# Attention with a forget gate and a SwiGLU FFN in one kernel: the first 256 queries of batch 0 ahead of the rest, and its row sums turned by TensorE

## The chip, the core and the metric

The kernel runs on one core of a Trainium2 chip. A core has five engines with queues of their own: TensorE (PE in the profile; PEld is its weight load), VectorE (DVE), ScalarE (ACT), GpSimd (POOL) and SyncE (SP, which here only issues DMAs). Each queue is worked off in order, and engines wait for one another through semaphores. Sixteen DMA engines are shared by all queues. TensorE writes into PSUM, here eight banks of 128 x 512 floats.

The metric is the device time of the whole program in microseconds (us), as the median of several runs. A profile is one more execution, with its own time.

## The reference, cut to what matters

Eight batches of eight heads, 576 tokens, head size 64. Attention has a causal mask and a decay made of the cumulative sum of log f. The output of attention, 4608 tokens by 512, goes through an FFN of inner size 1536.

```python
scores = q @ k.T / 8
cum = np.cumsum(np.log(np.clip(f, 1e-4, 1.0)), axis=-1)
scores = np.where(causal, -1e9, scores + cum[..., :, None] - cum[..., None, :])
attn = np.exp(scores - max); attn = attn / (attn.sum(-1) + 1e-9)
x = (attn @ v).transpose(0, 2, 1, 3).reshape(4608, 512)
g = x @ w_gate
out = (g * sigmoid(g) * (x @ w_val)) @ w_out
```

## The kernel before

The order of all work on every queue is written out by hand. The unit is a *slot*: one bank of scores of one head. A head has four banks (`BANKS`), since only the causal blocks are computed: bank 0 holds queries 0 to 255 (384 columns in all), banks 1 to 3 the queries 256 to 575 (512, 384 and 320 columns). Head h, bank i is slot 4h + i, so 64 heads are 256 slots and a batch is 32. A dictionary `todo` maps a slot to functions and their arguments; the loop at the end calls them slot by slot, and after them as many matmuls of the FFN as the slot's share is.

- `load`, `cast`, `transposes` bring in a pair of heads: SP loads q, k and v as f32, POOL casts to bf16 (DVE casts v for the first five pairs), PE turns q and k with an identity (L131), ACT copies q and DVE copies k from PSUM into the tile `QK` (L136, L138). Three `QK` tiles rotate.
- The decay rides in four more rows of `QK`, so that the score matmul adds it. At the start `dec` is computed on DVE and ACT; ACT issues four small DMAs that write the rows of the first pair, and one that writes `dec` to DRAM, from where `rows` fetches those of later pairs (SP).
- `qk` (L151) makes a bank of scores on PE, ACT takes the exponential into `pt` (L157), POOL masks the diagonal block (L166). `pv` (L181) follows three slots later (`LAG`). The value tile has a column of ones, so row 64 of the result is the row sum. The results go from PSUM to `ev` (L192 on DVE, L194 on ACT).
- The division goes by groups of four heads. `collect` spreads a group's sums over 128 partitions by DMA (`sc`), `recip` takes the reciprocal on DVE, `back` writes it to DRAM (`rc_d`), `spread` reads it back to 64 partitions (`rb`), all issued on ACT's queue. `normalise` (L221) multiplies on DVE into `xT`, the FFN's input. For the last head of a group these stand 5, 10, 11, 16 and 21 slots (`NORM`, then one slot for each head) after that head's first slot plus `LAG`.
- `ffn_stream` works off nine tiles of 512 tokens: twelve times four matmuls for gate (`gp`, L235) and four for value (`vp`, L243), with Tanh on ACT (L238) and two products on DVE (L239, L246), then four output blocks of twelve matmuls (`fo`, L252), copied by ACT to `ot` and stored by SP. Its PSUM pool `ps_ffn` has four banks; `ps_s` has two, `ps_t` and `ps_o` one each. A tile has 144 matmuls and is spread over 32 slots; the first begins at slot 56.
- POOL issues the weight loads, which cast to bf16 on the way: gate and value in quarters at slots 8, 10, 16, 18 up to 34, the output weights in halves at 36 and 40.

Of the kernel before, what the change touches and what calls it, by code (L numbers as in the profile page):

```python
# [11 lines left out]
ALU = mybir.AluOpType  # L12
# [15 lines left out]
FEW = 5  # L28
NORM = 21
# [3 lines left out]
def kernel(ctx, tc, q, k, v, f, w_gate, w_val, w_out, out):  # L33
# [23 lines left out]
    ptp = ctx.enter_context(tc.tile_pool(name="ptp", bufs=3))  # L57
    evp = ctx.enter_context(tc.tile_pool(name="evp", bufs=3))
# [10 lines left out]
    NBUF = 3  # L69

    QK = [consts.tile([KR, 4, NB * P], BF16, name=f"QK{i}") for i in range(NBUF)]
# [10 lines left out]
    def load(p, nm, part=0):  # L82
# [8 lines left out]
        if part == 0:  # L91
            nat[nm, p] = natp.tile([P, NB, 2, D], F32, name="nat_v", tag="nat_v")
# [18 lines left out]
    def cast(p, nm):  # L111
        if nm == "v":
            b = p % NBUF
            vn = nat.pop(("v", p))
            eng = nc.vector if p < FEW else nc.gpsimd
            eng.tensor_copy(VB[b][:, : NB - 1, :, :D], vn[:, : NB - 1])
            eng.tensor_copy(VB[b][:LAST, NB - 1, :, :D], vn[:LAST, NB - 1])
            return
        nc.gpsimd.tensor_copy(  # L119
            BF[nm, p % 2][:QP].rearrange("p t h d -> p h t d"),  # L120
            nat.pop((nm, p)).rearrange("p h (t d) -> p h t d", d=D),
        )

    def transposes(p, nm):
        w_ = 0 if nm == "q" else 1
        src = BF[nm, p % 2].rearrange("p t h d -> p t (h d)")
        pool, tag = (ps_s, "s") if p < FEW else (ps_t, "t")
# [4 lines left out]
        for a in range(2):  # L132
            dst = QK[p % NBUF][:D, 2 * a + w_, :S].rearrange("p (c n) -> p c n", n=QT)
            sr = t[a * D : (a + 1) * D, :S].rearrange("p (n c) -> p c n", n=QT)
            if p == 0 or nm == "q":
                nc.scalar.activation(dst, sr, AF.Copy)  # L136
            else:
                nc.vector.tensor_copy(dst, sr)  # L138
# [3 lines left out]
    def qk(h, i):  # L142
        b, j = (h // 2) % NBUF, h % 2
        if i == 0:
            PT[h] = ptp.tile([P, PT_W], BF16, name="pt", tag="pt")
        pt = PT[h]
        pool, tag = (ps_ffn, "f") if h < 2 * FEW else (ps_s, "s")
# [10 lines left out]
        if i == 0:  # L158
            diag = pt[:, : 2 * QSPLIT].rearrange("p (n x) -> p n x", x=QSPLIT)[:, :, :P]
            pat = [[0, 2], [1, P]]  # L160
        else:
            kt, q0, w = [x for x in BANKS[i] if x[1] == x[0] * P][0]
            lo = off + sum(x[2] for x in BANKS[i][: [y[0] for y in BANKS[i]].index(kt)])
            m = min(P, w)
            diag, pat = pt[:, lo : lo + m], [[1, m]]
        nc.gpsimd.affine_select(  # L166
            out=diag, in_=diag, pattern=pat, compare_op=ALU.is_ge, fill=0.0, base=0, channel_multiplier=-1,
        )

    def pv(h, i):  # L170
# [3 lines left out]
        if i <= 1:  # L174
            pool, tag = (ps_t, "t") if half == 0 else (ps_o, "o")
# [4 lines left out]
        for n, (kt, q0, w) in enumerate(BANKS[i]):  # L180
            nc.tensor.matmul(  # L181
                o[:, q0 - q_lo : q0 - q_lo + w], VB[b][:, kt, j, :], PT[h][:, c : c + w],
# [3 lines left out]
        if last:  # L186
# [4 lines left out]
            if h < H + GH or half == 1:  # L191
                nc.vector.tensor_copy(dst, o[: D + 1, :q_n])  # L192
            else:
                nc.scalar.activation(dst, o[: D + 1, :q_n], AF.Copy)  # L194
            O.pop((h, half))
# [31 lines left out]

    def ffn_stream():
        for t in range(NMT):
            ts = slice(t * MT, (t + 1) * MT)  # L230
            for fc in range(KF):
                fs = slice(fc * P, (fc + 1) * P)
                g_ = ps_ffn.tile([P, MT], F32, name="gp", tag="f")
                for ko in range(KD):
                    nc.tensor.matmul(g_, wg[:, ko, fs], xT[:, ko, ts], start=(ko == 0), stop=(ko == KD - 1))  # L235
                    if ko == KD - 1:
                        th = fp.tile([P, MT], F32, name="th", tag="th")
                        nc.scalar.activation(th, g_, AF.Tanh, scale=0.5)  # L238
                        nc.vector.scalar_tensor_tensor(out=th, in0=th, scalar=1.0, in1=g_, op0=ALU.add, op1=ALU.mult)  # L239
                    yield t  # L240
                v_ = ps_ffn.tile([P, MT], F32, name="vp", tag="f")
                for ko in range(KD):
                    nc.tensor.matmul(v_, wv[:, ko, fs], xT[:, ko, ts], start=(ko == 0), stop=(ko == KD - 1))  # L243
                    if ko == KD - 1:
                        h_ = hp.tile([P, MT], BF16, name="hh", tag="hh")
                        nc.vector.tensor_mul(h_, th, v_)  # L246
                        hh[fc] = h_
                    yield t
            for ms in range(MT // P):
                o = ps_ffn.tile([P, DM], F32, name="fo", tag="f")  # L250
                for fc in range(KF):
                    nc.tensor.matmul(o, hh[fc][:, ms * P : (ms + 1) * P], wo[:, fc, :],  # L252
                                     start=(fc == 0), stop=(fc == KF - 1))
                    if fc == KF - 1:
                        ot = op_.tile([P, DM], F32, name="ot", tag="ot")
                        nc.scalar.activation(ot, o, AF.Copy, scale=0.5)  # L256
                        r0 = t * MT + ms * P
                        nc.sync.dma_start(out=out[r0 : r0 + P, :], in_=ot)
                    yield t


    with tc.tile_pool(name="ini", bufs=1) as ini:
        lf = ini.tile([BH, S], F32, name="lf")
        nc.scalar.dma_start(out=lf, in_=f.rearrange("b h s -> (b h) s"))
        for p in range(2):
            load(p, "q")
            load(p, "k")
            for part in range(3):
                load(p, "v", part)
        ident = consts.tile([P, P], BF16, name="ident")  # L270
        make_identity(nc, ident[:, :])
        zero = ini.tile([BH, S], F32, name="zero")
        nc.gpsimd.memset(zero, 0.0)
        dec = ini.tile([BH, 2, 4, S], BF16, name="dec")
        nc.vector.memset(dec[:, 0, 1:], 1.0)
        nc.vector.memset(dec[:, 1, 0], 1.0)
        for nm in "qk":
            for i in range(2):
                nc.gpsimd.memset(BF[nm, i][QP:], 0.0)
        for i in range(NBUF):  # L280
            nc.gpsimd.memset(QK[i][:, 1::2, S:], 0.0)
            nc.gpsimd.memset(VB[i][:, :, :, D:], 1.0)
            nc.gpsimd.memset(VB[i][LAST:, NB - 1], 0.0)
        nc.vector.tensor_scalar(out=lf, in0=lf, scalar1=1e-4, scalar2=1.0, op0=ALU.max, op1=ALU.min)
        nc.scalar.activation(lf, lf, AF.Ln)
        cum = ini.tile([BH, S], F32, name="cum")
        nc.vector.tensor_tensor_scan(out=cum, data0=lf, data1=zero, initial=0.0, op0=ALU.add, op1=ALU.add)
        nc.scalar.activation(dec[:, 0, 0], cum, AF.Copy, scale=8.0)
        nc.vector.tensor_scalar_mul(dec[:, 1, 1], cum, -8.0)
# [3 lines left out]
        nc.vector.tensor_sub(dec[:, 1, 3], r1, dec[:, 1, 2])  # L293

        load(2, "q")
        load(2, "k")
        for r in range(4):
            nc.scalar.dma_start(
                out=QK[0][D + r : D + r + 1, :, :S], in_=dec[0:2, :, r]
            )  # L300
        nc.scalar.dma_start(out=dec_dram, in_=dec)
    fp = ctx.enter_context(tc.tile_pool(name="fp", bufs=3))
    hp = ctx.enter_context(tc.tile_pool(name="hp", bufs=14))
# [7 lines left out]

    for h in range(BH):
        for i in range(NSLOT):
            at(NSLOT * h + i, qk, h, i)
    for h in range(BH):
        s0 = NSLOT * h
        for i in range(NSLOT):
            at(s0 + i + LAG, pv, h, i)
        if h % GH == GH - 1:
            g = h // GH  # L320
            at(s0 + 5 + LAG, collect, g)
            at(s0 + 10 + LAG, recip, g)
            at(s0 + 11 + LAG, back, g)
            at(s0 + 16 + LAG, spread, g)
            for j in range(GH):
                at(s0 + NORM + LAG + j, normalise, g * GH + j)

    for p in range(NP):
        s0 = 2 * NSLOT * p
        for n, (nm, part) in enumerate((("q", 0), ("k", 0), ("v", 0), ("v", 1), ("v", 2))):  # L330
            if p > 2 or (p == 2 and nm == "v"):
                at(s0 - 24 + n + n // 2, load, p, nm, part)
        if p > 0:
            at(s0 - 10, rows, p)
        at(s0 - 11, cast, p, "q")
        at(s0 - 7, cast, p, "k")
        at(s0 - 4, cast, p, "v")
        at(s0 - 7, transposes, p, "q")
        at(s0 - 3, transposes, p, "k")
    def weights(t, src, lo, hi, cols):  # L340
        if cols:
            nc.gpsimd.dma_start(out=t[:, :, lo:hi], in_=src.rearrange("(ko p) n -> p ko n", p=P)[:, :, lo:hi])
# [57 lines left out]
```

The softmax here doesn't subtract the row's maximum and nothing guards it: scores larger than these inputs give would overflow.

## Time and profile before

| | |
|---|---|
| median of 5 runs | 457.51 us (455.73 to 457.89) |
| profiled execution: its own time | 456.28 us |
| its span, first to last instruction | 454.5 us |
| mean granted TensorE clock | 0.959 |
| PE busy | 412.4 us (91%) |
| DVE, ACT, POOL busy | 285.5, 264.3, 177.9 us (63%, 58%, 39%) |
| DMA | 54.01 MB, mean 119 GB/s |

"Busy" is the time in which an engine had an instruction in work. Matmuls overlap one another, so a PE that is busy is not a PE at its peak. The profile also has the span cut into 40 equal slices with a digit of busy tenths for each engine, windows of chosen length with busy time, granted TensorE clock and DMA share, the chain of waits that ended last, and groups of like instructions with the mean duration of one.

The costliest groups, with the number of instructions and the mean of one:

| line, engine, operation | count | mean |
|---|---|---|
| L157 ACT, exponential into pt | 256 | 503 ns |
| L166 POOL, mask of a diagonal block | 256 | 349 ns |
| L235, L243, L252 PE, FFN matmuls of 512 columns | 3 x 432 | 379 to 381 ns |
| L239, L246 DVE, the two FFN products | 2 x 108 | 686, 684 ns |
| L138 DVE and L136 ACT, k and q into QK | 62, 66 | 753, 644 ns |
| L221 DVE, the division into xT | 64 | 795 ns |
| L131 PE, bf16 transposes | 192 + 192 | 236, 233 ns |

### The profile page before, as it was taken

The page shows a single profiled execution, that of the slowest core. Times are in us where ns is not written, and L with a number is a line of the kernel's source. Part 1 is how long each engine was busy: PE and PEld are TensorE (multiplying, and loading weights), DVE is VectorE, ACT ScalarE, POOL GpSimd, SP SyncE. Part 2 cuts the span into 40 slices and gives each one's busy share as a digit, 9 for nine tenths or more (in the row PEclk, how much of TensorE's full clock was granted, in tenths as well). Part 3 has the DMA queues.
Part 4 walks back from the last instruction along what each step waited for, and adds up shares of the span by engine and source line. Part 5 has one row for each costly group of instructions (what it writes and reads, how often), then busy time and mean ns, then how long its engine had stood idle before and what let it go on. Part 6 is the DMA issues. An engine that isn't in the chain of part 4 may idle for free.

```text
span 454.5 us, 7457 instructions
## 1 busy us (share of the span) xinstructions
PE 412.4 (91%) x2576; PEld 227.1 (50%) x2576; DVE 285.5 (63%) x452; ACT 264.3 (58%) x522; POOL 177.9 (39%) x404
## 2 busy tenths in 40 slices
PE   0685586999999999999999999999999999999996
PEld 0353353545555555555555555555555544444442
DVE  6355535787478747874788467846784585670760
ACT  2875463666677667666766677667766622332331
POOL 9476753353544454445454545454544200000000
PEclk9989555999999999999999999999999999999999
DMA  9899999440694068506850775077204113101002
GB/s 203 177 235 210 200 237 220 103 95 23 183 211 107 18 187 206 112 12 192 194 124 8 197 189 127 3 202 187 52 3 123 34 44 100 46 1 69 25 1 92
DMA packets 69417, 54.01 MB, mean 119 GB/s; under 512 B 45188, under 2 KB 63620, under 8 KB 68292
## 3 DMA queue, kind: packets, MB, share of 16 engines
q1 hardware_dynamic: 57516, 38.33, 34.2%
q10 hardware_dynamic: 6072, 10.49, 9.9%
q0 software_dynamic: 5792, 4.72, 6.5%
q8 instruction: 20, 0.33, 0.3%
q14 instruction: 17, 0.14, 0.1%
HBM read 47.90 MB, written 10.17 MB: 128 GB/s over the span
## 4 chain that ended last, share of the span: by engine, by line
PE 78%; DMA 9%; DVE 8%; ACT 2%; issue 2%; SPq 0%; ACTq 0%; DVEq 0%
PE fo L252 21%; PE gp L235 19%; PE vp L243 18%; PE o L181 8%; PE s L151 8%; PE tp L131 4%; DVE QK L138 3%; DMA rb<-rc_d 3%; DMA rc_d<-rc 3%; DVE xT L221 1%; DMA sc<-ev 1%; DVE th L239 1%; DMA nat_q<-in_q_dram 1%; DVE ev L192 1%; ACT QK L136 1%
## 5 line engine op out<-in xcount | busy, mean ns | idle before, releaser
L157 ACT ACTIVATE pt<-s 128x384 bf16<-128x384 f32 (+2 forms) x256 | 126.2, 503 | 82.1 <-PE s L151 70.8
L166 POOL TENSOR_SCALAR_AFFINE_SELECT pt<-pt 128x128 bf16<-128x128 bf16 (+2 forms) x256 | 88.7, 349 | 183.6 <-ACT pt L157 182.6
L235 PE MATMUL gp<-xT,wg 128*128 128x512 bf16 x432 | 120.0, 381 | 0.5 <-DVE th L239 0.5
L243 PE MATMUL vp<-xT,wv 128*128 128x512 bf16 x432 | 119.6, 380 | 0.2 <-DVE hh L246 0.2
L239 DVE SCALAR_TENSOR_TENSOR th<-th,gp 128x512 f32<-128x512 f32 x108 | 74.1, 686 | 64.3 <-ACT th L238 63.8
L181 PE MATMUL o<-pt,VB 128*128 128x320 bf16 (+4 forms) x448 | 92.0, 276 | 21.2 <-DVE QK L138 7.6
L252 PE MATMUL fo<-wo,hh 128*128 128x512 bf16 x432 | 104.4, 379 | 0.0
L151 PE MATMUL s<-QK 68*128 68x320 bf16 (+4 forms) x448 | 92.4, 279 | 5.6 <-ACT QK L136 3.1
L238 ACT ACTIVATE th<-gp 128x512 f32<-128x512 f32 x108 | 64.3, 596 | 50.8 <-PE gp L235 43.1
L246 DVE TENSOR_TENSOR hh<-th,vp 128x512 bf16<-128x512 f32 x108 | 73.9, 684 | 8.3 <-PE vp L243 1.1
L151 PEld LDWEIGHTS <-QK 68*128 68x128 bf16 x448 | 45.6, 105 | 48.0 <-ACT QK L136 3.4
L181 PEld LDWEIGHTS <-VB 128*128 128x128 bf16 x448 | 41.5, 102 | 48.4 <-issue 12.1
L192 DVE COPY ev<-o 65x320 f32<-65x320 f32 (+1 forms) x76 | 35.3, 471 | 43.5 <-PE o L181 42.8
L221 DVE TENSOR_TENSOR xT<-ev,rb 64x576 bf16<-64x576 f32 x64 | 50.9, 795 | 14.6 <-DMA rb<-rc_d 13.5
L252 PEld LDWEIGHTS <-hh 128*128 128x128 bf16 x432 | 40.7, 97 | 38.3
L235 PEld LDWEIGHTS <-wg 128*128 128x128 bf16 x432 | 41.0, 98 | 37.4 <-issue 1.3
L243 PEld LDWEIGHTS <-wv 128*128 128x128 bf16 x432 | 40.3, 98 | 36.3 <-issue 1.0
L138 DVE COPY QK<-tp 64x576 bf16<-64x576 bf16 x62 | 46.7, 753 | 17.4 <-PE tp L131 16.7
L136 ACT ACTIVATE QK<-tp 64x576 bf16<-64x576 bf16 x66 | 42.5, 644 | 6.0 <-DMA QK<-dec 4.2
L256 ACT ACTIVATE ot<-fo 128x512 f32<-128x512 f32 x36 | 21.5, 597 | 35.4 <-PE fo L252 31.9
L119 POOL CAST b_q<-nat_q 96x768 bf16<-96x768 f32 x32 | 27.0, 844 | 0.1
L131 PE MATMUL tp<-ident,b_q 128*128 128x128 bf16 x192 | 17.9, 236 | 10.1 <-POOL b_q L119 10.1
(37 smaller groups left out, 151.9 us busy)
## 6 DMA issues: line engine op xcount, KB each, us to landing
nat_q<-in_q_dram SPq DMA_DIRECT2D x32, 288.0 KB
nat_k<-in_k_dram SPq DMA_DIRECT2D x32, 288.0 KB
rb<-rc_d ACTq DMA_DIRECT2D x16, 576.0 KB
out_dram<-ot SPq DMA_DIRECT2D x36, 256.0 KB
nat_v<-in_v_dram SPq DMA_DIRECT2D x64, 128.0 KB
wg<-in_moe_w_gate_dram POOLq DMA_DIRECT2D x4, 384.0 KB, 8.6
wv<-in_moe_w_val_dram POOLq DMA_DIRECT2D x4, 384.0 KB, 8.6
wo<-in_moe_w_out_dram POOLq DMA_DIRECT2D x2, 768.0 KB, 15.4
```

What stands on the lines that cost most here:

```text
L138: nc.vector.tensor_copy(dst, sr)
L151: nc.tensor.matmul(s[:, c : c + w], QK[b][:, 2 * j + 1, kt * P : (kt + 1) * P], QK[b][:, 2 * j, q0 : q0 + w], start=True, stop=True,)
L157: nc.scalar.activation(pt[:, off : off + c], s[:, :c], AF.Exp, scale=0.125)
L166: nc.gpsimd.affine_select(out=diag, in_=diag, pattern=pat, compare_op=ALU.is_ge, fill=0.0, base=0, channel_multiplier=-1,)
L181: nc.tensor.matmul(o[:, q0 - q_lo : q0 - q_lo + w], VB[b][:, kt, j, :], PT[h][:, c : c + w], start=(i <= 1 and n == 0), stop=(last and n = ...
L221: nc.vector.tensor_mul(xT[a * D : (a + 1) * D, (h % H) // 2, b0 : b0 + S], E[g][:D, j], RB[g][:, j])
L235: nc.tensor.matmul(g_, wg[:, ko, fs], xT[:, ko, ts], start=(ko == 0), stop=(ko == KD - 1))
L238: nc.scalar.activation(th, g_, AF.Tanh, scale=0.5)
L239: nc.vector.scalar_tensor_tensor(out=th, in0=th, scalar=1.0, in1=g_, op0=ALU.add, op1=ALU.mult)
L243: nc.tensor.matmul(v_, wv[:, ko, fs], xT[:, ko, ts], start=(ko == 0), stop=(ko == KD - 1))
L246: nc.vector.tensor_mul(h_, th, v_)
L252: nc.tensor.matmul(o, hh[fc][:, ms * P : (ms + 1) * P], wo[:, fc, :], start=(fc == 0), stop=(fc == KF - 1))
```

## The change

- **Order of slots in batch 0.** Bank 0 of all eight heads comes first, in slots 0 to 7; then banks 1 to 3 head by head, slots 8 to 31. From head 8 on all is as before. For the first eight slots `pv` follows two slots later (`LAG0`), scores go to `ps_ffn`, and the exponentials to tiles of their own (`pt0p`, four buffers), with two mask instructions instead of one.
- **Row sums of batch 0.** They no longer go by DMA. For each half of a head, `turn` makes PE turn the row of sums into columns (two or three small f32 transposes), DVE takes their reciprocals, and `turn_back`, one slot later, makes PE spread them over 64 partitions; DVE multiplies them into `xT`. The sums take the last columns of a PSUM bank of `ps_ffn`, the spread values its first ones.
- **FFN tiles.** The first tile of 512 tokens becomes two of 256. A tile begins in the slot in which its tokens are ready, and its columns are spread evenly up to the beginning of the next: slots 12 to 36, 37 to 84, then 85 to 116 and so on.
- **Row sums of later batches.** `collect`, `recip`, `back`, `spread` and `normalise` stand 2, 6, 7, 11 and 15 slots after the last `pv` of the group; before they stood 2, 7, 8, 13 and 18 slots after it.
- **Start and loads.** q and k of three pairs are loaded first, then v. One tile `QKA` holds four buffers, and four DMAs on SP's queue write the decay rows of all eight heads of batch 0. Memsets, casts and transposes of the first pairs are put in a new order, and a one-element exponential is run early. In later batches loads come 20 slots ahead instead of 24 and `rows` 16 slots ahead instead of 10.
- **Weights.** Gate and value in quarters at slots 1, 2, 4, 5, 7, 8, 10 and 11; output weights in quarters at 15, 18, 21 and 24.
- `hp` has 13 buffers instead of 14, `nat_v` two instead of three; DVE casts v for the four pairs of batch 0.

```diff
-FEW = 5
-NORM = 21
+LAG0 = 2
+    pt0p = ctx.enter_context(tc.tile_pool(name="pt0p", bufs=4))
+    eap = ctx.enter_context(tc.tile_pool(name="eap", bufs=3))
-    NBUF = 3
+    NBUF = 4
+    FB = H // 2
+    QKA = consts.tile([KR, NBUF, 4, NB * P], BF16, name="QK")
+    QK = [QKA[:, i] for i in range(NBUF)]
...
+    def turn(h, half):
+        n = QSPLIT if half == 0 else S - QSPLIT
+        RS[h, half] = rs = ps_ffn.tile([P, MT], F32, name="rs", tag="f")
+        RCP[h, half] = rc = rp.tile([P, 3], F32, name="rcp", tag="rcp")
+        ea = EA[h, half]
+        for c in range(0, n, P):
+            w, x = min(P, n - c), SUMS + c // P
+            nc.tensor.transpose(rs[:w, x : x + 1], ea[D : D + 1, c : c + w], ident_f[D : D + 1, D : D + 1])
+        full = n // P
+        nc.vector.reciprocal(rc[:, :full], rs[:, SUMS : SUMS + full])
+        if n % P:
+            nc.vector.reciprocal(rc[: n % P, full : full + 1], rs[: n % P, SUMS + full : SUMS + full + 1])
+
+    def turn_back(h, half):
+        n = QSPLIT if half == 0 else S - QSPLIT
+        rc, rs, ea = RCP.pop((h, half)), RS.pop((h, half)), EA.pop((h, half))
+        for c in range(0, n, P):
+            w = min(P, n - c)
+            nc.tensor.transpose(
+                rs[:D, c : c + w], rc[:w, c // P : c // P + 1].to_broadcast([w, D]), ident_f[:w, :w]
+            )
+        j, q0 = h % 2, QSPLIT * half
+        nc.vector.tensor_mul(xT[j * D : (j + 1) * D, h // 2, q0 : q0 + n], ea[:D, :n], rs[:D, :n])
...
+    TILES = [(0, QSPLIT), (QSPLIT, MT - QSPLIT)] + [(t0, MT) for t0 in range(MT, N_TOK, MT)]
...
+        for r in range(4):
+            nc.sync.dma_start(
+                out=QKA[D + r : D + r + 1, :, :, :S].rearrange("r b (j w) s -> r (b j) w s", w=2), in_=dec[:H, :, r]
+            )
...
+    def slot(h, i):
+        if h >= H:
+            return NSLOT * h + i
+        return h if i == 0 else H + (NSLOT - 1) * h + i - 1
...
+        if h < H:
+            for half, s in enumerate((slot(h, 0) + LAG0, slot(h, NSLOT - 1) + LAG)):
+                at(s + 1, turn, h, half)
+                at(s + 2, turn_back, h, half)
+                ready[half] = s + 3
+        elif h >= H and h % GH == GH - 1:
+            g = h // GH
+            s = slot(h, NSLOT - 1) + LAG
+            at(s + 2, collect, g)
+            at(s + 6, recip, g)
+            at(s + 7, back, g)
+            at(s + 11, spread, g)
+            for j in range(GH):
+                at(s + 15 + j, normalise, g * GH + j)
+            ready[1 + h // H] = s + 15 + GH
...
     for c in range(4):
         lo, hi = c * DFF // 4, (c + 1) * DFF // 4
-        at(NSLOT * (2 + 2 * c), weights, wg, w_gate, lo, hi, True)
-        at(NSLOT * (2 + 2 * c) + 2, weights, wv, w_val, lo, hi, True)
-    for c in range(2):
-        at(NSLOT * (9 + c), weights, wo, w_out, c * KF // 2, (c + 1) * KF // 2, False)
+        at(1 + 3 * c, weights, wg, w_gate, lo, hi, True)
+        at(2 + 3 * c, weights, wv, w_val, lo, hi, True)
+    for c in range(4):
+        at(15 + 3 * c, weights, wo, w_out, 3 * c, 3 * c + 3, False)
...
+    begin = [ready[0], ready[1]]
+    begin += [ready[1 + (t0 + n - 1) // S] for t0, n in TILES[2:]]
...
+        while nxt is not None and nxt[0] + 1 < len(begin) and s >= begin[nxt[0]]:
+            t = nxt[0]
+            if t != t_now:
+                t_now, done = t, 0.0
+            if done >= work[t] * (s + 1 - begin[t]) / (begin[t + 1] - begin[t]):
+                break
+            done += nxt[1]
+            nxt = next(ffn, None)
```

## The prediction, made before the changed kernel was run

> **What bounds the kernel now.** I read the 40 slices first, then the windows of the slow stage, then the chain of waits in order of time. In the slices, TensorE (PE) is nearly full from about 80 us to the end, and before that it is neither full nor at full clock:
>
> ```profile
> PE   0685586999999999999999999999999999999996
> PEclk9989555999999999999999999999999999999999
> DMA  9899999440694068506850775077204113101002
> ```
>
> One digit is 11.4 us. The seven slices that matter are the first ones: DMA at its limit, PE at 0 to 8 tenths, clock down to 5 tenths. The windows (engine busy us of 10, then clock, DMA share, GB/s) say the same in numbers:
>
> ```profile
> 50.00:60.00 10.00, 6.42 (x34) 3.68 (x33) 6.51 (x11) 5.00 (x10) 6.04 (x14) 0.50 1.22 210
> 60.00:70.00 10.00, 8.58 (x52) 5.62 (x50) 2.90 (x5) 5.47 (x11) 5.72 (x15) 0.50 1.17 233
> 70.00:80.00 10.00, 5.61 (x24) 2.85 (x23) 5.78 (x9) 3.93 (x8) 3.13 (x7) 0.50 1.11 223
> 80.00:90.00 10.00, 10.00 (x65) 5.58 (x64) 7.28 (x12) 6.85 (x15) 3.59 (x10) 1.00 0.35 88
> ```
>
> The chain (start, length, what) names the waits of that stage, in its answer for the first 128 us:
>
> ```profile
> 32.56 6.30 DMA sc<-ev
> 39.18 5.40 DMA rc_d<-rc
> 44.61 5.72 DMA rb<-rc_d
> 50.42 0.76 DVE xT L221
> ...
> 57.21 6.06 DMA rc_d<-rc
> 63.30 7.99 DMA rb<-rc_d
> 71.38 0.76 DVE xT L221
> ...
> 76.31 1.71 PE gp L235 x4
> ...
> 119.62 0.34 PE tp L131 x6
> ...
> 123.97 0.86 PE gp L235 x4
> ```
>
> Batch 0's row sums go out and come back by three small DMAs per group of four heads, each taking 5.4 to 8 us while the DMA engines are full; 31.5 us of the chain are these five. The first FFN matmul starts at 76.3 us, the second FFN tile at 124.0. From there PE alone sets the pace: the full chain has the next tile's first gp at
>
> ```profile
> 169.77 0.86 PE gp L235 x4
> ```
>
> so a batch is 45.8 us (169.77 - 123.97). That is 144 matmuls of 0.216 (0.86/4) = 31.1, 8 heads of 1.40 (the chain's pieces of 0.14 to 0.22 for four banks of scores and four of values) = 11.2, eight groups of transposes of 0.34 = 2.7: 45.0. This stage has nothing to give; the change must earn its time before 124.0.
>
> **The change part by part, in slots.** A slot is one bank of scores. Before, tile 0 is spread over slots 56 to 87 and tile 1 starts at slot 88. After, the half tile of tokens 0 to 255 fills slots 12 to 36, the half of 256 to 511 fills 37 to 84, and the 512-token tiles start at 85, 117 and so on, 32 slots each as before. So slot 85 after is slot 88 before, at 124.0. What follows is 454.5 - 124.0 = 330.5, plus the 0.75 head that three slots hold: 0.75 x (1.40 + 0.34) = 1.3. I sum the time to slot 85 in four pieces.
>
> *To the first score matmul: 16.3.* Before it is at 14.96. The decay rows of all eight heads are now four SP issues (ACT's four took 3.47 in all), behind fourteen loads in SP's queue; the last waits for DVE's last decay operation (ends 11.6 before) and for the three issues ahead. With a landing of 0 to 4.1 us (the lf load: issued 0.82, used 4.96) it is there at 14.6 to 18.7; I take 16.3. Behind these issues SP holds the V loads of pairs 2 and 3, used ten us later. The Exp table load (1.28) moves from behind the first score into a wait, so the first exponential ends about 17.4.
>
> *Slots 0 to 11: to 33.* GpSimd decides. Between the first exponential and head 7's mask it runs 16 selects of 0.357 = 5.7, two blanks of 0.20 + 0.63 + 0.46 = 2.6, two casts of 0.83 = 1.7, and four weight issues of 0.78 = 3.1, which now stand among the selects: 13.1, so 30.5. ACT has 7.9 and DVE 11.8 in that time. Head 7 then goes through PV 0.3, copy 0.42, turn, reciprocal (0.26 at most), turn back and product (half of 0.75): with hand-overs 2.5. First gp at 33.0 against 76.3. Bounds 31 to 36.
>
> *Slots 12 to 36: 34.* PE: 96 half-width matmuls of 0.108 = 10.4 and 24 of 0.216 = 5.2; 25 slots of 2 x 0.177 = 8.9; three transposes groups 1.0; six small f32 turns a head, 48 in all. No row has these. The nearest is the bf16 transpose: 0.34/6 = 0.057 in a row, 0.236 as a single record. I take 0.06 for a one-column turn and 0.14 for a turn back, 4.8 in all; the bounds are 2.7 and 11.3. Sum 30.3. To it 2.5 for the eight turns that wait behind DVE's copy (0.48, with the one operation of 0.38 before it) with everything on PE behind them, and 1.0 for a clock that starts low. ACT's sum is 20 and DVE's 20, so both are hidden. Range 31 to 40. The weights: issued from slots 1 to 24 instead of 8 to 40; at 8.6 us from issue to landing (the page's median) wv's last quarter is there near 44, used near 50; wo's quarters at 47 to 59, used from 56 to 60. The loads of batch 1 compete less, since SP now waits at the rows of pair 4 until PE has passed slot 13; behind that wait stand the loads of pair 5, used 16 slots later.
>
> The page "TensorE: Matmul & The Clock Gate", section "Part 4: PE-mode transpose", of the Trainium skill puts a transpose at some 275 ns in a kernel and says that it does not count as activity for the clock. This speaks against the change: 48 such turns would be 13.2 us and the final sum 8.4 us more. In this trace six transposes take 0.34 us at full clock, so I do not use it.
>
> *Slots 37 to 84: 50.* Here only half a tile lies under 48 slots of attention. PE has 48 x 0.354 + 15.6 + 12 x 0.34 = 36.7. ACT has more: 48 exponentials of 0.503 = 24.1, 12 copies of 0.644 = 7.7, nine of 0.376 = 3.4, twelve Tanh of 0.38 (between 0.376 at 256 and 0.436 at 320 columns) = 4.6, two of 0.597, and some 2.2 groups of three DMA issues (0.50 + 0.33 + 0.46) = 2.9: 43.9. Each of the 27 copies and Tanh stands behind a PE piece of its own slot, at 0.14 to 0.34 a wait: 6 more. Range 45 to 58. The rows of groups 2 and 3 still take the three DMAs, with four slots each instead of five; at 1.04 us a slot that is 4.2 us, and the DMA engines are no longer full.
>
> Sum: 33 + 34 + 50 + 330.5 + 1.3 = 448.8, 5.7 less than the span of 454.5. The profiled execution took 456.28; the runs' median is 457.51. I take the 5.7 off the median: 451.8, told as 452.
>
> **The rivals.** *A cold clock in slots 37 to 84 (slower).* Before, the clock stayed at 0.50 through 50 to 80 us although PE was 56 to 86% busy; here PE needs 36.7 of 50 at full clock. If a wait of three us puts it down for 34 us, as before, these do 17 us of the work, and the other 19.7 go at 73% in 27: 61 us, the span 459.8, the median 463. It decides once this stage passes 55.7 (124.0 - 1.3 - 67), that is with half of it cold. Against it: from 80 us a dense PE has clock 1.00 at once, and no full DMA queue is left to make the long wait. The skill's page named above ("Part 1: The HAM clock gate") has the clock return after some 3.4 us of sustained activity and fall after an idle window as long. The trace agrees where FFN starts (76.3, full from 80), but 30 us at 56 to 86% busy did not bring it back. By the rule the stage would be 50, by those rows 61.
>
> *Tighter row sums (about the same).* From the issue of rb to the first product there are four slots, five before. In the FFN output part it was 5.06 (issue 157.05, product 162.11), so 3.6 is left. If rb lands just in time for 5.06, each of seven odd groups waits 1.4 on DVE, behind which stand the copies that free PE's output bank: up to 9.8. I price 7: median 458.8. Against it: PE waited 2.7 us on DVE in all of 125 to 360.
>
> *The early start fails (same).* If wo's quarters land at 15.4 instead of 8.6, the fo matmuls wait 6: 457.8.
>
> *Near the sums (faster).* Slots 12 to 36 in 31, 37 to 84 in 45: 440.8 span, median 444.
>
> **How the numbers follow.** Forecast 0.42 (own range 446 to 458), near the sums 0.20, cold clock 0.18, tighter sums 0.10, late weights 0.10. A measurement can tell 0.3% (456.1 to 458.9). Faster: 0.36 + 0.20 + 0.06 = 0.62. Same: 0.04 + 0.09 = 0.13. Slower: 0.18 + 0.02 + 0.05 = 0.25. The range is 442 to 464: most of both outer cases, some tenth left out at each end.
>
> **What would show it.** First s near 16, first gp near 33, the tile of 512 (full-width gp) near 117 instead of 124.0; 45.8 from one full tile to the next; no sc, rc_d or rb before 65 us. Between 67 and 117 ACT should be about 88% busy and the clock at 1.00. Wrong if gp starts after 40, if the turns take over 0.2 each, if the clock stands at 0.50 after 45 us, or if DVE waits for rb in every group.

## The result and the profile after

The changed kernel takes 455.71 us, the median of 51 runs (452.87 to 458.04); the kernel before, in the runs beside it, 457.10 (91 runs). The ratio is 0.9966, 95% interval 0.9958 to 0.9975: a gain of a third of one per cent, where 1.2% was forecast. The profiled execution took 456.00 us with a span of 453.2, so its steps can be set beside the forecast's sum of 448.8.

The same rows of the 40 slices as were shown of before, now of the changed kernel:

```profile
PE   2399999877799999999999999999999999999996
...
PEclk9999999999899999999999999999999999999999
DMA  9899936483835275627462756274614023101002
```

TensorE (PE) is full from the third slice, where before it was from the eighth. But slices 8 to 11 (about 79 to 125 us) fall back to 7 and 8 tenths, and the clock row has a dip in slice 11. The DMA engines are at their limit for five slices instead of seven.

Windows cut at the forecast's own steps (the last two at the first gp matmul of the second half tile, 72.54 us, and of the first full tile, 121.80; stretch, us, busy us with the number of instructions on PE, PEld, DVE, ACT and POOL, clock, DMA share, GB/s):

```profile
0.00:19.50 19.50, 3.26 (x24) 2.24 (x25) 13.21 (x18) 6.60 (x9) 10.96 (x22) 1.00 0.93 206
19.50:37.80 18.30, 17.27 (x101) 11.78 (x102) 10.58 (x28) 9.69 (x21) 14.47 (x36) 1.00 1.01 170
37.84:72.54 34.70, 33.50 (x279) 23.26 (x278) 20.30 (x60) 19.96 (x44) 15.01 (x38) 1.00 0.80 152
72.54:121.80 49.26, 39.12 (x364) 28.68 (x362) 31.26 (x61) 37.16 (x85) 30.29 (x73) 0.99 0.62 147
```

| step | forecast | measured | difference |
|---|---|---|---|
| to the first score matmul | 16.3 | 19.53 | +3.2 |
| slots 0 to 11, to the first gp (37.84) | 16.7 | 18.3 | +1.6 |
| slots 12 to 36, to the first gp of the second half tile (72.54) | 34 | 34.7 | +0.7 |
| slots 37 to 84, to the first full-width gp (121.80) | 50 | 49.3 | -0.7 |
| the rest | 331.8 | 331.4 | -0.4 |
| span | 448.8 | 453.2 | +4.4 |

In the second line POOL has only 14.47 us of 18.3, and PE has 17.27: the queue that was to decide is not the fullest one. Cut in two, the line shows PE and POOL close together up to 28 us, and PE nearly full only behind that:

```profile
19.50:28.00 8.50, 7.72 (x52) 5.99 (x53) 4.86 (x10) 5.83 (x12) 7.14 (x18) 1.00 0.69 134
28.00:37.80 9.80, 9.55 (x49) 5.79 (x49) 5.72 (x19) 3.85 (x9) 7.33 (x19) 1.00 1.29 201
```

(The clock of 1.00 up to 38.8 us is what is written before the first record of a change. The durations tell otherwise: six transposes take 0.84 us at 21.4 us, 0.50 at 115.0.) In the line of slots 37 to 84 ACT, which was to be the bound at 88%, is busy for 37.16 of 49.26, 75%.

The chain of waits in order of time (start, length, what), where each of the late steps shows:

```profile
16.38 2.90 DMA QK<-dec
...
22.84 0.78 POOL b_q L122
23.61 0.77 POOL b_k L122
24.38 0.85 POOL wg L438
25.24 0.61 POOL pt L175 x2
...
27.70 0.29 POOL pt L175
...
30.46 0.32 PE s L157 x2
30.78 0.43 PE rs L239 x2
31.20 0.30 PE rs L228 x2
31.50 0.43 PE o L193 x2
...
42.59 0.39 ACT th L289
...
43.01 0.43 DVE th L290
...
43.53 0.42 DVE hh L298
43.95 0.41 DVE ea L213
...
44.41 0.31 PE rs L228 x3
...
94.33 5.41 DMA rb<-rc_d
...
111.35 6.51 DMA rb<-rc_d
```

This is what stands here. The decay rows land at 19.28. From 20.6 to 28 us the chain lies on POOL, as was forecast, and from 28 us on it lies on PE, whose slot is a turn back (0.43), a turn (0.30), values (0.43) and scores (0.32), 1.48 us. In slots 12 to 36 a turn (L228) stands behind DVE's copy to `ea`, which stands behind both FFN products, which stand behind a Tanh: 1.8 us from 42.59 to the turn at 44.41. And in slots 37 to 84 the chain goes twice through the spread of the reciprocals, `rb`, though that was to be the rival of another stage.

### The profile page after: what moved, and what is told of

It reads as the page before. It is cut to its first block, busy times and chain, and to the rows that moved or that the text cites. A ratio compares the mean times of both kernels' runs of the same rounds, so it can differ in the third digit from the quotient of the medians.

```text
span 453.2 us, 7863 instructions
## 1 busy us (share of the span) xinstructions
PE 417.1 (92%) x2752; PEld 239.1 (53%) x2752; DVE 291.0 (64%) x504; ACT 264.4 (58%) x537; POOL 183.4 (40%) x418
## 4 chain that ended last, share of the span: by engine, by line
PE 68%; DVE 15%; DMA 6%; issue 4%; ACT 4%; POOL 2%; ACTq 0%; POOLq 0%; DVEq 0%
PE fo L305 18%; PE gp L287 16%; PE vp L296 15%; PE o L193 8%; PE s L157 7%; DMA rb<-rc_d 4%; DVE hh L298 3%; DVE QK L141 3%; DVE xT L269 3%; DVE th L290 3%; PE tp L134 3%; ACT th L289 1%; PE rs L239 1%; ACT pt L163 1%; ACT QK L139 1%
## 5 line engine op out<-in xcount | busy, mean ns | idle before, releaser
L287 PE MATMUL gp<-xT,wg 128*128 128x512 bf16 (+1 forms) x480 | 124.7, 361 | 0.5 <-DVE xT L269 0.5
L296 PE MATMUL vp<-xT,wv 128*128 128x512 bf16 (+1 forms) x480 | 124.2, 358 | 0.9 <-DVE th L290 0.5
L290 DVE SCALAR_TENSOR_TENSOR th<-th,gp 128x512 f32<-128x512 f32 (+1 forms) x120 | 75.7, 631 | 64.2 <-ACT th L289 63.4
L193 PE MATMUL o<-pt,VB 128*128 128x320 bf16 (+4 forms) x448 | 87.9, 266 | 13.3 <-DVE QK L141 6.4
L289 ACT ACTIVATE th<-gp 128x512 f32<-128x512 f32 (+1 forms) x120 | 66.4, 554 | 56.7 <-PE gp L287 49.9
L298 DVE TENSOR_TENSOR hh<-th,vp 128x512 bf16<-128x512 f32 (+1 forms) x120 | 75.5, 629 | 6.3 <-PE vp L296 0.9
L157 PEld LDWEIGHTS <-QK 68*128 68x128 bf16 x448 | 44.7, 101 | 46.2 <-issue 5.6
L269 DVE TENSOR_TENSOR xT<-ev,rb 64x576 bf16<-64x576 f32 x56 | 45.4, 810 | 30.4 <-DMA rb<-rc_d 29.8
L296 PEld LDWEIGHTS <-wv 128*128 128x128 bf16 x480 | 45.3, 98 | 36.6 <-issue 2.7
L193 PEld LDWEIGHTS <-VB 128*128 128x128 bf16 x448 | 37.8, 98 | 32.8 <-PE s L157 9.5
L213 DVE COPY ev<-o 65x320 f32<-65x320 f32 (+1 forms) x60 | 28.7, 479 | 5.1 <-PE o L193 4.4
L122 POOL CAST b_k<-nat_k 96x768 bf16<-96x768 f32 x32 | 29.1, 909 | 1.1 <-DMA nat_k<-in_k_dram 1.1
```

Of the source, the lines that this page charges most:

```text
L157: nc.tensor.matmul(s[:, c : c + w], QK[b][:, 2 * j + 1, kt * P : (kt + 1) * P], QK[b][:, 2 * j, q0 : q0 + w], start=True, stop=True,)
L193: nc.tensor.matmul(o[:, q0 - q_lo : q0 - q_lo + w], VB[b][:, kt, j, :], PT[h, half][:, c : c + w], start=(i <= 1 and n == 0), stop=(last a ...
L269: nc.vector.tensor_mul(xT[a * D : (a + 1) * D, (h % H) // 2, b0 : b0 + S], E[g][:D, j], RB[g][:, j])
L287: nc.tensor.matmul(g_[:, :n], wg[:, ko, fs], xT[:, ko, ts], start=(ko == 0), stop=(ko == KD - 1))
L289: nc.scalar.activation(th[:, :n], g_[:, :n], AF.Tanh, scale=0.5)
L290: nc.vector.scalar_tensor_tensor(out=th[:, :n], in0=th[:, :n], scalar=1.0, in1=g_[:, :n], op0=ALU.add, op1=ALU.mult)
```

## The experiments

All are edits of the changed kernel. Ratios are to the kernel before, on the same chip, with their 95% intervals; spans and steps are of one profiled execution each.

| run | median us | ratio | first s / gp / full gp at |
|---|---|---|---|
| the changed kernel | 455.71 | 0.9966 (0.9958 to 0.9975) | 19.53 / 37.84 / 121.80 |
| e1, dummy matmuls | 454.89 | 0.9961 (0.9944 to 0.9979) | 19.65 / 37.83 / 124.70 |
| e2, decay rows on two queues | 454.93 | 0.9958 (0.9943 to 0.9973) | 17.97 / 36.28 / 121.82 |
| e3, first halves not divided | 452.46 | 0.9903 (0.9886 to 0.9920) | 18.98 / 34.15 / 120.50 |
| e4, old distances | 466.02 | 1.0202 (1.0183 to 1.0220) | 19.54 / 37.85 / 129.87 |
| e5, spread in six slots | 451.86 | 0.9876 (0.9855 to 0.9896) | 19.09 / 37.42 / 118.50 |
| e6, one first tile | 457.90 | 1.0010 (0.9989 to 1.0032) | 18.91 / 67.36 / 123.96 (second tile) |
| e7, e2 and e5 | 449.53 | 0.9837 (0.9819 to 0.9855) | 17.67 / 35.80 / 117.57 |
| e8, batch 0 not divided | 446.63 | 0.9770 (0.9757 to 0.9784) | 18.68 / 33.87 / 114.26 |
| e9, old distances and loads | 465.31 | 1.0175 (1.0128 to 1.0222) | 19.70 / 38.01 / 127.74 |
| e10, old loads | 453.74 | 0.9918 (0.9889 to 0.9946) | 18.74 / 37.04 / 121.51 |
| e11, e2 and spread in seven slots | 449.07 | 0.9824 (0.9791 to 0.9858) | 18.10 / 36.41 / 116.75 |

### Is it the cold clock at the start? (e1)

```diff
         transposes(1, "q")
+        spin(28)
         cast(0, "v")
         transposes(1, "k")
+        spin(40)
```

`spin(n)` issues n matmuls of 128 columns on the identity.

> The changed kernel plus 68 matmuls of the identity with itself (128 columns, result unused) in the gap on PE before the first score matmul, 28 of them before the last transposes of k and 40 after. Theory A (slots 0 to 11 are bound by PE at half clock): the clock is full by about 18 us, a pair of bank-0 score matmuls takes 0.16 instead of 0.32 us, the first gp comes near 33.5 instead of 37.8, the whole 3 to 4.5 us earlier. Rival B (GpSimd's masks and weight issues bind slots 0 to 11): first gp not before 37, the whole within 1 us. Rival C (the clock falls again as soon as only transposes and small matmuls follow): full clock at 18 us, half again by 25, gain under 1.5 us.

The clock came up early and did not stay. Windows of this run:

```profile
12.00:16.00 4.00, 3.88 (x40) 3.64 (x38) 3.92 (x7) 0.15 (x1) 2.59 (x5) 1.00 1.17 268
16.00:22.80 6.80, 3.44 (x49) 2.75 (x46) 1.84 (x5) 2.75 (x7) 2.10 (x8) 0.99 0.55 138
22.80:39.90 17.10, 16.47 (x90) 10.75 (x91) 10.35 (x29) 7.95 (x18) 13.10 (x31) 0.51 1.17 194
```

A dense burst gave the full clock at 16 us. In the next 6.8 us PE was half idle, and the clock went down at 22.6 and stayed down until 39.7, although PE was busy for 16.47 us of the last window's 17.10. The first gp came at 37.83, to within 0.02 us where it was. So this burst bought nothing. Of slots 0 to 11 only the first 3 us ran at full clock, in the stretch where the chain of the changed kernel lies on POOL; what a full clock in all of these slots would be worth isn't shown, and the question above stays open.

### What the start costs (e2)

```diff
+    def decay(r, eng):
+        eng.dma_start(
+            out=QKA[D + r : D + r + 1, :, :, :S].rearrange("r b (j w) s -> r (b j) w s", w=2), in_=dec[:H, :, r]
+        )
...
+        for r in range(2):
+            decay(r, nc.scalar)
         transposes(0, "k")
...
-        for r in range(4):
-            nc.sync.dma_start(
-                out=QKA[D + r : D + r + 1, :, :, :S].rearrange("r b (j w) s -> r (b j) w s", w=2), in_=dec[:H, :, r]
-            )
+        for r in range(2, 4):
+            decay(r, nc.sync)
```

> The changed kernel with the decay rows' four DMAs split: rows 0 and 1, whose data is ready at 9.4 us, are issued by ACT as soon as it has them, rows 2 and 3 stay on SP. Theory A: the first score matmul waits 4.8 us for these DMAs alone, so it comes near 17 instead of 19.5, and all behind it moves by as much: first gp near 35.3, the whole 2 to 2.7 us earlier. Rival B: the first mask or the casts of pair 3 on GpSimd, or the weights' landing, hold the later slots: first score earlier, first gp moved by less than 1 us.

The first score matmul came 1.56 us earlier, and so did the first gp. But the first full-width gp stood at 121.82 (121.80). Most of the gain was gone before the spreads: the second half tile began at 72.26 us instead of 72.54. The trace's clock records, one for each stretch of the same granted clock, show why. The clock came up at 39.98 us, in the changed kernel at 38.77, so 3.7 us of the first half tile ran at half clock instead of 0.9, which is worth half the difference, 1.4 us. The last 0.3 went in slots 37 to 84, where the two spreads stand in the chain (6.64 and 6.24 us). The median, 0.8 us lower, is not set apart from the changed kernel by the intervals. What the start loses is real: the three runs with split rows have their first score at 17.67 to 18.10 us, the others at 18.68 to 19.70, which also shows that one profile's start is known to about a microsecond only.

### What the turns cost (e3 and e8)

```diff
+    def keep(h, half):
+        n = QSPLIT if half == 0 else S - QSPLIT
+        ea = EA.pop((h, half))
+        j, q0 = h % 2, QSPLIT * half
+        nc.vector.tensor_scalar_mul(xT[j * D : (j + 1) * D, h // 2, q0 : q0 + n], ea[:D, :n], 0.01)
...
-                at(s + 1, turn, h, half)
-                at(s + 2, turn_back, h, half)
+                if half in (0,):
+                    at(s + 2, keep, h, half)
+                else:
+                    at(s + 1, turn, h, half)
+                    at(s + 2, turn_back, h, half)
```

e8 has `(0, 1)` in the place of `(0,)`.

> The changed kernel without the division of the first 256 queries of batch 0: turn, reciprocals and turn_back of half 0 are left out, and DVE multiplies by a constant instead. 32 f32 turns fewer, all in slots 0 to 12. Theory A (PE binds these slots, at half clock): 8 heads x 0.73 us = 5.8 less PE work there; GpSimd then binds: first gp near 33 to 34. Rival B (GpSimd binds all along): first gp moves by under 1 us, for the shorter tail of head 7 alone. If the clock is full earlier too, f32 turns were what kept it down.

> The changed kernel without any division of batch 0 (both halves: no turn, no reciprocal, no turn back; DVE multiplies by a constant). 80 f32 turns fewer. Theory A: slots 0 to 11 as with half 0 alone (first gp near 34.2); slots 12 to 36 lose 24 x 0.10 + 24 x 0.13 = 5.6 us of PE work and the eight waits for DVE's copy, so 30 to 31 instead of 37.3; what reaches the first full-width gp is less, since the waits for rb stand in between: 114 to 118. Rival B (slots 12 to 36 are bound by ACT or DVE): 34 or more.

The windows of e8 at the same steps:

```profile
18.70:33.90 15.20, 11.64 (x70) 7.89 (x71) 10.06 (x20) 9.54 (x21) 13.84 (x34) 1.00 0.98 165
33.90:64.40 30.50, 27.96 (x229) 20.39 (x228) 17.11 (x43) 19.47 (x43) 16.17 (x40) 1.00 1.04 197
64.40:114.30 49.90, 39.74 (x366) 28.94 (x364) 31.27 (x61) 37.29 (x85) 31.00 (x75) 0.97 0.62 145
```

Without turns slots 0 to 11 take 15.2 us (in e3 too: 34.15 - 18.98), and POOL is busy for 13.84 of them: now GpSimd decides, as was forecast. With turns it is 18.3, PE having 17.27. So the turns of the first halves cost 3.1 us, where they were held to be hidden but for the last. Slots 12 to 36 take 30.6 instead of 34.7: with the turns of the second halves they take 4.1 more, and the forecast had 4.8 + 2.5 = 7.3 for them. (e8 runs the first 2.6 us of this stage at half clock, the changed kernel 0.9; an estimate with the same clock is 4.9.) In all the median is 9.1 us lower without the division by turns (455.71 - 446.63), where the whole change gained 1.4. The two stages hold 7.2 of the 7.9 us between the spans; 0.8 more is an earlier first score, which lies ahead of all turns.

The clock is as late as with turns: it came up at 36.5 in e8 and at 38.8 in the changed kernel, 2.6 and 0.9 us behind the first gp. So it isn't the turns alone that hold it down.

### What the spread of later batches costs (e5), and the old distances (e4)

e5 gives `rb` six slots to land instead of four, by taking the steps ahead of it earlier:

```diff
-            at(s + 6, recip, g)
-            at(s + 7, back, g)
-            at(s + 11, spread, g)
+            at(s + 5, recip, g)
+            at(s + 6, back, g)
+            at(s + 9, spread, g)
```

e4 puts back the five steps' old distances, and with them the tiles' first slots (88, 120 and so on):

```diff
-            at(s + 6, recip, g)
-            at(s + 7, back, g)
-            at(s + 11, spread, g)
+            at(s + 7, recip, g)
+            at(s + 8, back, g)
+            at(s + 13, spread, g)
             for j in range(GH):
-                at(s + 15 + j, normalise, g * GH + j)
-            ready[1 + h // H] = s + 15 + GH
+                at(s + 18 + j, normalise, g * GH + j)
+            ready[1 + h // H] = s + 18 + GH
```

> The changed kernel with recip, back and spread of batches 1 to 7 moved forward to 5, 6 and 9 slots behind the last values (6, 7 and 11 before), normalise left at 15: rb has six slots instead of four, 5.3 us instead of 3.6 at the 0.89 us a slot of this stage, against a landing of 5.4 to 6.5. Theory A (waiting for rb costs PE and then the clock between 98 and 122 us): the two DVE waits of 1.0 and 4.1 us go below 1.5 in sum, the first full-width gp comes near 117.5 instead of 121.8, the whole 3 to 5 us earlier. Rival B (other DMAs of this stage, sc and rc_d, only take its place): recip or ACT waits for them, first full-width gp not before 120.5, the whole within 1 us.

> The changed kernel with the row-sum steps of batches 1 to 7 at their old distances (2, 7, 8, 13, 18 slots behind the last values instead of 2, 6, 7, 11, 15), so full tiles begin at slots 88, 120 and so on. Theory A (the two waits for rb at 99 and 117 us cost about 4 us): they shrink to under 1 us each, slot 85 is passed some 3 us earlier, but the tile that begins there starts three slots later, so the whole is within 1.5 us of the changed kernel. Rival B (the waits are covered by ACT anyway): the full tile begins 2.7 us later and the whole is 1 to 3 us slower.

The waits of DVE and PE between 75 and 125 us (engine, instruction, line, what it waited for: us in all, times, the longest), first of the changed kernel:

```profile
DVE xT L269 <- DMA rb<-rc_d: 5.1, 2, 4.1
...
PE o L193 <- DVE ev L213: 3.3, 2, 2.3
```

and then of e5:

```profile
DVE xT L269 <- DMA rb<-rc_d: 1.5, 2, 0.9
...
PE o L193 <- DVE ev L213: 1.0, 1, 1.0
```

The wait of 5.1 us on DVE is passed on to PE because the copies that free the output bank (`ev`) stand behind the product on DVE's queue. With six slots 3.6 us of it are gone, slots 37 to 84 take 46.2 us instead of 49.3, the first full-width gp comes at 118.50 instead of 121.80, and the clock stays at 1.00 from 38.7 us to the end: behind the second wait of the changed kernel the clock had gone down as well. The first full tile, which began at half clock there, takes 45.6 us instead of 46.7. The median falls by 3.9 us, for a change of three numbers.

e4 missed both expectations by far: 10.3 us slower. Its first full tile begins 8.1 us later and the rest takes 3.8 longer (335.2 for 331.4). Three slots of 0.9 us are 2.7 of the first; the waits of DVE for `rb` there are as long as in the changed kernel (1.0 and 3.9 us; a spread of 6.72 stands in the chain), one wait for a store of the output (7.62 us) has joined them, and PE is busy for 19.83 of the 29 us from 100 on. In the rest, the first full tile takes 48.6 us instead of 46.7 and three others 46.8 instead of 45.6, and between 130 and 400 us four waits stand there that the changed kernel hasn't:

```profile
PE o L193 <- POOL pt L175: 5.1, 4, 1.3
```

### Do loads and row sums collide? (e9 and e10)

A rival was that the row sums of e4 meet the loads of the next batch on the DMA engines, since the change had moved both together. e10 puts back the old times of the loads, e9 these and the old distances of e4.

```diff
-                at(s0 - 20 + n + n // 2, load, p, nm, part)
-            at(s0 - 16, rows, p)
+                at(s0 - 24 + n + n // 2, load, p, nm, part)
+            at(s0 - 10, rows, p)
```

> The changed kernel with the old distances of the row sums of batches 1 to 7 (2, 7, 8, 13, 18 slots) and also the old times of the loads (24 slots ahead, decay rows 10 ahead). With the old distances alone the median was 466.0 and the first full tile began at 129.9. If the distance of the loads and stores from the row sums' transfers is what made that run slow (transfers that meet on the DMA engines), the old pair fits together again: first full tile at 122 to 125, median 454 to 459. If the later products themselves cost the time (their place between the FFN's operations on VectorE), the loads change nothing: 464 to 468.

> The changed kernel with the old times of the loads alone. If spacing and loads were moved together because they collide otherwise, this run is slower than the changed kernel, by 3 to 10 us (459 to 466). If the loads don't matter for the row sums, it is within 1.5 us of it (454 to 457).

The collision falls: e9 is as slow as e4, and e10 is no slower than the changed kernel but, if anything, 2 us faster (the intervals, 0.9889 to 0.9946 and 0.9958 to 0.9975, do not meet). In e10 the first full tile takes 45.56 us to the next instead of 46.71. That is the clock: in the changed kernel the first 2.3 us of this tile ran at half clock, in e10 none of it. Nor do the new times of the loads cost this by themselves, since e5 has them and takes 45.57. In e9 PE stands idle around both waits for `rb`, and after each the clock is at half; windows of it:

```profile
105.00:107.00 2.00, 0.08 (x1) 0.11 (x2) 1.94 (x4) 0.00 (x0) 1.84 (x5) 1.00 0.26 62
107.00:109.00 2.00, 1.74 (x9) 0.96 (x9) 1.99 (x5) 0.87 (x2) 0.27 (x1) 0.61 0.61 126
...
123.00:125.00 2.00, 0.00 (x0) 0.00 (x0) 1.97 (x3) 0.06 (x1) 1.73 (x3) 0.88 0.74 168
125.00:127.00 2.00, 0.73 (x4) 0.43 (x5) 1.96 (x4) 0.22 (x1) 0.00 (x0) 0.50 0.08 19
127.00:129.00 2.00, 2.00 (x8) 0.96 (x7) 1.05 (x2) 1.14 (x3) 0.41 (x1) 0.50 0.16 57
```

Twice DVE works for 4 us on products and copies that queued up behind `rb`, and PE waits for them; then PE goes on at half clock. It looks like the changed kernel's second wait, larger and twice. Why three slots make so much of it, and why POOL's mask is late once a batch, was not settled.

### Does the division into two half tiles pay? (e6)

```diff
-    TILES = [(0, QSPLIT), (QSPLIT, MT - QSPLIT)] + [(t0, MT) for t0 in range(MT, N_TOK, MT)]
+    TILES = [(t0, MT) for t0 in range(0, N_TOK, MT)]
...
-    begin = [ready[0], ready[1]]
-    begin += [ready[1 + (t0 + n - 1) // S] for t0, n in TILES[2:]]
+    begin = [ready[1]]
+    begin += [ready[1 + (t0 + n - 1) // S] for t0, n in TILES[1:]]
```

> The changed kernel with the first FFN tile left whole: 512 tokens, begun at slot 37 and spread to slot 84. Undoes the two halves alone. Theory A (PE work is only moved: slots 12 to 36 become bound by ACT at 0.87 us a slot, 22 us instead of 37; slots 37 to 84 then hold a whole tile, PE 1.09 a slot, 53 plus the waits for rb of about 2): slot 85 at 38 + 22 + 55 = 115 to 118, the whole 4 to 7 us EARLIER than the changed kernel, so the halves cost time. Rival B (the early half fills PE time that is idle otherwise, as meant): slot 85 at 125 or later, the whole 3 us or more later.

With one tile of 512 tokens that fills slots 37 to 84, the kernel is as slow as before (1.0010, 0.9989 to 1.0032), some 2 us behind the changed one. The halves pay, but little: the FFN starts 29.5 us earlier with them (37.84 for 67.36), and nearly all of that is given back before the full tiles. Neither expectation had the size: the first tile begins at 67.36 where Theory A had 60, and the next at 123.96, 2.2 us behind the changed kernel, in the direction of Rival B. One part of the giving back is seen in e6, which waits for `rb` once in this stage (3.8 us) and not twice (5.1); how the rest divides was not tried. The clock stays low for longer in e6: six transposes take 0.85, 0.85 and 0.83 us at 51.8, 57.2 and 63.0, and 0.50 at 67.0. It came up at 64.5, ahead of the first gp.

### The pieces together (e7 and e11)

e7 is e2 and e5 in one. e11 is e2 with the steps 1, 4, 5 and 8 slots after the last `pv`, so that `rb` has seven slots.

```diff
-            at(s + 2, collect, g)
-            at(s + 5, recip, g)
-            at(s + 6, back, g)
-            at(s + 9, spread, g)
+            at(s + 1, collect, g)
+            at(s + 4, recip, g)
+            at(s + 5, back, g)
+            at(s + 8, spread, g)
```

(from e7 to e11)

> The two edits together: decay rows split between ACT and SP, and rb two slots earlier. Theory A (the 1.6 us won at the start was lost again in waiting for rb, which hangs on DMAs and not on the start): both gains add once rb is early, first gp 36.3, first full-width gp near 116, the whole 5 to 6 us faster than the changed kernel. Rival B (something else between 75 and 98 us, such as the loads of q, takes the 1.6 back): no better than rb alone.

> Two rows of the decay on ScalarE's queue, and collect, reciprocal, back and spread 1, 4, 5 and 8 slots after the last value matmul of a group, so that the spread has seven slots (the changed kernel has four; with six and the same start the median was 449.5). If the wait for the spread values still costs what the trace of the six-slot version shows on VectorE (1.5 us), up to 1 us is gained: 448.5 to 449.5. If the transfers before it (sums to 128 partitions, reciprocals to DRAM) are now cut short, VectorE or ScalarE waits for these: 450 to 453.

The gains add up: e7 is 1.6% below the kernel before (449.53 us) and 2.3 us below e5. Of the 1.4 us by which it starts ahead of e5, 0.8 are left at the second half tile (71.45 for 72.26) and 0.9 at the first full-width gp. That the wait for `rb` had absorbed the gain of e2 does not follow from it: in e2 most of that gain was gone before this wait, by the clock. e11, at 449.07 us, is within e7's interval; DVE's wait for `rb` in this stage is down to one of 0.7 us, and the last step of the way has little left to give. Both beat both kernels.

## Why the prediction was right in direction and wrong in size

**First score matmul (16.3, was 19.5): mis-sized.** The mechanism was named, four issues in a row on one queue behind the last decay operation, but priced at 3.0 us from the end of `dec` to the last issue and 1.7 for the landing. The queue's rows of the changed kernel:

```profile
11.63 0.40 SPq L89 DMA_DIRECT2D nat_k<-in_k_dram  x1
12.12 4.94 SPq L368 DMA_DIRECT2D QK<-dec  x4
17.16 0.94 SPq L98 DMA_DIRECT2D nat_v<-in_v_dram  x2
```

Four issues took 4.94 us (0.86, 0.71, 2.40 and 0.68), where ACT's four took 3.47 before. `dec` ended at 12.35 instead of 11.6, the last issue 4.7 us behind that (17.06), and its row landed 2.2 later (19.28), past the upper bound of 18.7: 0.7, 1.7 and 0.5 us more than forecast, and 0.25 to the matmul. What made the third issue so long is open. e2 brings back 1.6 of the 3.2.

**Slots 0 to 11, "GpSimd decides" (33.0, was 37.8): the step that failed.** It is true of the kernel without turns (e3 and e8: 15.2 us, POOL 13.84). With them it holds up to 28 us; from there PE decides, and it runs at half clock: 1.48 us a slot. The forecast costed PE in this stage at nothing but head 7's tail; the turns' 3.1 us were not hidden. Together with the start this is 4.8 us, more than the whole miss of the span (4.4).

**Slots 12 to 36 (34, was 34.7): near, but by luck.** The turns were priced at 7.3 us (4.8 on PE and 2.5 in waits) and cost 4.1; what is left was priced at 26.7 and took 30.6 in e8. The two errors nearly cancel. A one-column turn is a step of 0.10 in the chain (three in 0.31) and a turn back 0.13 (three in 0.39), so the prices of 0.06 and 0.14 were near. 24 of each are 5.5 us; that the stage is only 4.1 longer with them fits the idle time that PE has without them. In e8 PE was busy for 27.96 us, where the sum has 25.5, and idle for 2.5: 1.5 of it waiting for the output weights, 0.9 behind DVE's copies. The Trainium skill's page "TensorE: Matmul & The Clock Gate" puts a bf16 transpose of 128x128 at some 275 ns in one kernel ("Part 4: PE-mode transpose"). The small f32 steps here are 100 and 130 ns, and the 48 turns of this stage made it 4.1 us longer with all their waits, where an estimate with the page's figure is 13.2.

**Slots 37 to 84 (50, was 49.3): near, and bound by another thing than was said.** ACT's sum of 43.9 plus 6 of waits was too high. ACT's groups by shape in this stage:

```profile
L163 ACT ACTIVATE pt<-s 128x384 bf16<-128x384 f32 x24 | 11.8, 492 | 5.1 <-PE s L157 4.8
L163 ACT ACTIVATE pt<-s 128x512 bf16<-128x512 f32 x13 | 7.7, 595 | 1.5 <-PE s L157 1.3
L139 ACT ACTIVATE QK<-tp 64x576 bf16<-64x576 bf16 x12 | 7.7, 643 | 0.2
L163 ACT ACTIVATE pt<-s 128x320 bf16<-128x320 f32 x12 | 5.2, 437 | 0.0
L289 ACT ACTIVATE th<-gp 128x256 f32<-128x256 f32 x12 | 4.6, 382 | 0.0
```

With two smaller groups (3.4 and 1.8) the durations add up to 42.2 us, near the forecast's 41.0 without the DMA issues, but ACT is busy for 37.16: the records of instructions one after another overlap at their ends, so a sum of durations is above the time that they take. (The forecast's 27 waits also don't match its own list of 12 + 9 + 12 = 33 copies and Tanh.) Without most of the waits for the spread the stage takes 46.2 us (e5), 3.8 less than forecast; the waits, which were put at nothing, bring back 3.0. So this number, too, came out by two errors of opposite sign.

The rival "tighter row sums" named the mechanism, a landing of some 5 us against a shorter distance, and also the way it goes on (DVE, then the copies, then PE). It was priced in the full tiles, seven times 1.4 us (its 3.6 us for four slots is the 5.06 less a slot of 1.43; four fifths of 5.06 are 4.0). There DVE does wait, 3.3 to 4.1 us in each of five groups, but PE is hardly held up: the full tiles take 45.6 us. In slots 37 to 84 a slot lasts 0.93 us (slots 40 to 60 in 18.5), four slots are 3.7 us, and `rb` lands in 5.4 to 6.5. Its cost to the kernel is some 3.9 us of the median (e5), with the half clock that follows it, and this is the place that the forecast passed over with "4.2 us, and the DMA engines are no longer full".

**The cold clock as a rival** did not come in slots 37 to 84: half clock for the last 1.1 us only, and for the first 2.3 of the full tile. It was in slots 0 to 11, for which it had no price.

**The rest (331.8, was 331.4)** and the early weights were right: no wait for the weights stands in the changed kernel's chain.

The errors sum to +5.5 us up to slot 37 and -1.1 after it. Of the forecast gain of 5.7 us in the span, 1.3 were left. What failed is the start and GpSimd as the bound of slots 0 to 11; the two stages behind came out near the forecast without its mechanism.

## What to carry to other kernels

When a step is made shorter, distances that are counted in slots shrink with it: work out each DMA's allowance as slots times the duration of a slot in that very stage, not in the steady one. A small operation that is "hidden" needs a named engine with spare time at the clock that holds there: at half clock PE had 17.3 of 18.3 us filled. Undoing the parts one by one and then adding the two that pay found 6.6 us (455.71 to 449.07), more than the change itself had earned.

## What the runs showed of the hardware

The clock. In the changed kernel PE was busy for 17.27 of 18.30 us with scores, values, transposes and turns, and the clock stayed at half until 38.8, 0.9 us behind the first FFN matmul; in e6 it stayed so until 64.5 with PE busy 23.5 of 24.5 us, and in e1 from 22.6 to 39.7. A full stream of FFN matmuls is not what it takes: in e6 it came up 2.9 us ahead of the first of them, and in e7 it was full from 25.1 to 28.5, in slots 0 to 11. What brings it up was not found. In the clock records of all these traces, the stretches between two changes are multiples of 3.41 us (3.41, 6.83, 10.24, 13.65, 17.07, 68.27). The moment of the rise explains how long slots 12 to 36 take where nothing else in them was changed: 34.2 us and half of the time that they spend at half clock (0.9 us: 34.7; 1.8 in e1: 35.1; 3.7 in e2: 36.0; 3.9 in e10: 36.1). Steps of two profiles can differ by over a microsecond from this alone.

The other way a short gap is enough; windows of the changed kernel:

```profile
117.00:120.50 3.50, 1.24 (x9) 0.75 (x10) 2.57 (x4) 1.44 (x4) 2.27 (x5) 1.00 1.09 208
120.50:124.00 3.50, 3.50 (x17) 1.91 (x16) 2.62 (x4) 1.34 (x3) 1.06 (x2) 0.53 0.51 154
```

One wait of 2.26 us, in a stretch in which PE was busy for 1.24 of 3.5 us, was followed by half clock for 3.4 us (120.7 to 124.1). The Trainium skill's page "TensorE: Matmul & The Clock Gate" ("Part 1: The HAM clock gate") has the clock come back after some 3.4 us of sustained activity. That agrees with the 3.4 us here, amid FFN matmuls, and not with the 16 to 24 us of busy PE at half clock at the start.

A small DMA isn't small for its queue: of the four that write decay rows, 18 KB in 16 stretches of one partition each, three held SP's queue for 0.68 to 0.86 us and one for 2.40.
